# A written-out order for the first part of a fused recurrence and gated-MLP kernel: the state's matmuls as a step of their own, a read of the banks in place of a drain, 48-row loads

## The chip, the cores and the metric

The kernel runs on one core of a Trainium2 chip. The metric is device microseconds (us) of one execution; lower is better. Shown are the median of three runs and one execution taken with the hardware profiler.

## The reference

A gated linear recurrence over time feeds a gated MLP.

```python
B, H, S, D = 4, 8, 768, 48
for t in range(S):
    kt, vt, rt = k[:, :, t], v[:, :, t], r[:, :, t]
    cur = einsum('bhd,bhe->bhde', u[None] * kt, vt)
    y[:, :, t] = einsum('bhd,bhde->bhe', rt, state + cur)
    state = w[None, :, :, None] * state + einsum('bhd,bhe->bhde', kt, vt)
x = y.transpose(0, 2, 1, 3).reshape(B * S, H * D)          # 3072 x 384
gate = 1 / (1 + exp(-(x @ w_gate)))                         # 384 x 1536
out = (gate * (x @ w_val)) @ w_out                          # 1536 x 384
```

## The kernel before

**Tiling.** Time is cut into 12 chunks of 64 steps; a chunk has two groups of heads (`GROUPS`, numbered 0 to 23: chunk 0 is groups 0 and 1, chunk 1 is groups 2 and 3, and so on). Two chunks make a token tile of 512 columns, 256 from each. The MLP's 1536 hidden units come in 12 slices f of 128. A weight arrives as 64-bit words; ScalarE and VectorE turn it into a 32-bit value, which is split into a high and a low part, so each product of the MLP takes three matmuls.

**Steps.** In the first part (groups 0 to 7 and 14 items of MLP work) the string `START` gives the order of every step. Each engine has its own in-order queue, so the order in the string is the order on each engine. After it comes a loop over the rest, which this change touches only through the loads and through shared functions. A step's name is a letter and a number; the number is the group n, the slice f, or the item i. The names used here are these.

- SyncE's queue issues the loads: `L.n` channels (r and k of group n, 512 KB), `X.n` tokens (k and v, 400 KB), `W.f` weights (1152 KB, slice 0 in two halves), `F.n` six small copies (`fills`) that rearrange x inside SBUF.
- TensorE: `Z.n` scores, 64 small matmuls. `I.n` apply: from chunk 1 on 32 matmuls from the state (`from_state`), then 32 from the scores, into the same two banks. `O.n` the state's update, 32 matmuls. `U.i` up-projection of item i, `D.i` down-projection of item i, `tt` a table turned round.
- VectorE: `k`, `Rv` (scaled keys and queries), `K` (keep: scores under a mask into SBUF), `s` (add to the state), `l` (the low part of x), `j` (join the words of a weight slice, three instructions), `ov` (the low part of the weights), `Tv` (scaled token keys), `m` (gate times value), `qv` (the low part of h).
- ScalarE: `A` (bonus keys), `c`, `w` (scale the words, high part of the weights), `d` (decay the state), `h` (the high part of x), `g` (sigmoid), `H` (the high part of h), `tn`.
- GpSimd: the same as `Rv`, `Tv`, `ov`, `qv` under the names `R`, `T`, `o`, `q`.

Items 0 and 2 use weight slice 0, items 1 and 3 slice 1: items 0 and 1 work on the 256 columns of chunk 0, items 2 and 3 on those of chunk 1. Items 4 to 13 use slices 2 to 11 on all 512 columns. So U.0 needs the x of groups 0 and 1 and the copies F.0, and U.2 needs the x of groups 2 and 3 and the copies F.2.

**Buffers.** The ring of PSUM banks has three: an apply takes two, an up-projection takes two one after the other, and each waits for the readers of the bank's last tenant. The scores have one pair of banks. Channel loads rotate through three buffers.

**The drain.** In the first part an apply is `from_state`, then `nc.tensor.drain()`, then the matmuls from the scores. In the later part the next group's scores and the outer products stand between the two halves, and two one-column copies of the banks into `seen` (line 374) set the order.

Of the kernel before, what the change touches and what calls it, by code (L numbers as in the profile page):

```python
# [9 lines left out]
F32 = mybir.dt.float32  # L10
# [21 lines left out]
GROUPS = [(c, g) for c in range(NC) for g in (1, 0)]  # L32
# [4 lines left out]
HALF, FIRST = 2, 8  # L37
# [1 line left out]


START = """
L.0 tc A.0 tk ti.1 tp W.0 X.0 k.0 Rv.0 c0.0 ti.0 c0.1 L.1 j0.1 A.1 Z.0 K.0 tt L.2 k.1 I.0 Rv.2 A.2
R.1 X.1 tn h.0 T.0 X.3 Z.1 k.2 T.1 l.0 L.3 K.1 O.0 s.0 j0.0 W.1 A.3 I.1 w0.1 o0v.1 h.1 l.1 L.4 R.3
w0.0 c.1 X.2 F.0 Z.2 K.2 W.2 o0.0 O.1 s.1 j.1 Tv.3 X.6 U.0 g.0 c.2 m.0 I.2 k.3 w.1 W.4 W.7 ov.1 d.2
T.2 O.2 h.2 l.2 X.4 s.2 H.0 Z.3 K.3 A.4 q.0 k.4 R.4 c.4 j.2 U.1 g.1 I.3 O.3 L.7 L.5 m.1 d.3 h.3 H.1
l.3 A.5 D.0 w.2 R.5 Z.4 T.4 s.3 K.4 F.2 U.2 k.5 g.2 m.2 q.1 D.1 H.2 U.3 g.3 Z.5 j.4 m.3 X.5 I.4 O.4
W.3 L.6 T.5 H.3 d.4 R.6 X.7 ov.2 h.4 q.3 q.2 c.3 K.5 W.5 s.4 w.4 l.4 U.4 j.3 D.2 g.4 m.4 A.6 H.4 D.3
ov.4 qv.4 w.3 I.5 O.5 d.5 W.6 h.5 c.5 D.4 k.6 ov.3 l.5 c.6 s.5 U.5 A.7 g.5 j.5 w.5 U.6 g.6 j.6 w.6
ov.5 c.7 Z.6 m.5 m.6 K.6 U.7 H.5 qv.5 W.9 g.7 j.7 H.6 D.5 qv.6 o.6 I.6 Tv.6 w.7 W.8 k.7 d.6 D.6 O.6
m.7 Rv.7 H.7 s.6 h.6 c.8 l.6 ov.7 U.8 g.8 q.7 F.6 j.8 c.9 j.9 D.7 w.8 U.9 g.9 ov.8 Z.7 W.11 m.9 w.9  # L50
U.10 H.9 m.8 W.10 H.8 qv.8 D.8 g.10 o.9 K.7 q.9 D.9 m.10 I.7 c.11 j.11 c.10 H.10 qv.10 D.10 h.7 T.7
d.7 j.10 w.10 O.7 l.7 s.7 U.11 w.11 ov.10 g.11 ov.11 U.12 m.11 H.11 F.7 g.12 m.12 q.11 H.12 q.12 D.11
U.13 g.13 D.12 m.13 H.13 q.13
"""


# [1 line left out]
def rwkv_then_moe(ctx: ExitStack, tc: tile.TileContext, wd, ch, tk, rt, ut, wt, rk0, vn0, wd0, out):  # L58
    nc = tc.nc
# [19 lines left out]
    def one_bank():  # L79
        return ring.tile([P, 512], F32, name="ring")  # L80
# [168 lines left out]
    xt, dec, ga, yb, kv = {}, {}, {}, {}, {}  # L249
    seen = const.tile([112, 2], F32, name="seen")  # L250
# [94 lines left out]

    def keep(n):
        sc, t = ga.pop(n), score[n % 2]
# [6 lines left out]
        for m, at in ((0, 0), (1, 256))[: 1 if n >= FIRST else 2]:  # L354
# [233 lines left out]
    def finish(i):  # L588
# [29 lines left out]
    for step in START.split():  # L618
        name, _, arg = step.partition(".")
# [16 lines left out]
    n = FIRST  # L636
# [51 lines left out]
    with tc.If(bad != 0):  # L688
        with ExitStack() as g:
# [3 lines left out]
            st = gp.tile([P, NP, B, D], F32, name="st")  # L693
# [18 lines left out]
            with tc.For_i(0, NC) as c:  # L712
                for p in range(NP):
                    nc.sync.dma_start(
                        out=rkc[:, p].rearrange("q a b i -> q (a b i)"),
                        in_=rk0[bass.ds(c, 1), p].rearrange("o q x -> (o q) x"),
                    )
                with tc.For_i(0, C) as i:
                    for lo, side in ((0, 1), (64, 0)):
# [18 lines left out]
                    for lo in (0, 64):  # L738
                        y = one_bank()
# [11 lines left out]
                    out=xg[bass.ds(c, 1)].rearrange("o q p t -> (o q) p t"),  # L751
                    in_=yc.rearrange("q p b i -> q p (b i)"),
# [119 lines left out]
```

## Time and profile before

| | us |
|---|---|
| median of three runs | 541.75 |
| lowest and highest | 540.87, 541.93 |
| the profiled execution | 540.73 |
| its span, first to last instruction | 538.9 |
| TensorE busy in the span | 518.4 (96%) |
| VectorE busy in the span | 216.4 (40%) |
| bytes moved by DMA | 48.03 MB |

A span is counted from the first instruction; the profiled execution's own time is 1.8 us more. Rows name a line of the kernel, an engine and the tiles by the program's names: `ring<-dec,state` is a matmul from the state, `ring<-score,toks` one from the scores, `ring<-xt,wx` an up-projection, `acc<-h,wx` a down-projection, `xt<-ring,xt` on VectorE the low part of x.

### The profile page before, as it was taken

The page shows a single profiled execution, that of the slowest core. Times are in us where ns is not written, and L with a number is a line of the kernel's source. Part 1 is how long each engine was busy: PE and PEld are TensorE (multiplying, and loading weights), DVE is VectorE, ACT ScalarE, POOL GpSimd, SP SyncE. Part 2 cuts the span into 40 slices and gives each one's busy share as a digit, 9 for nine tenths or more (in the row PEclk, how much of TensorE's full clock was granted, in tenths as well). Part 3 has the DMA queues.
Part 4 walks back from the last instruction along what each step waited for, and adds up shares of the span by engine and source line. Part 5 has one row for each costly group of instructions (what it writes and reads, how often), then busy time and mean ns, then how long its engine had stood idle before and what let it go on. Part 6 is the DMA issues. An engine that isn't in the chain of part 4 may idle for free.

```text
span 538.9 us, 12058 instructions
## 1 busy us (share of the span) xinstructions
PE 518.4 (96%) x5268; PEld 425.6 (79%) x5268; DVE 216.4 (40%) x375; ACT 171.3 (32%) x354; POOL 174.8 (32%) x159
## 2 busy tenths in 40 slices
PE   2889999999999999999999999999999999999996
PEld 2778878788788887888888888888888887888885
DVE  7999989912343342432413414313414311111111
ACT  5485755522132322231332222312322212221121
POOL 3424022122814444244145144143242311111120
PEclk9999999999999999999999999999999999999998
DMA  8895705053022214220303402203400001100001
GB/s 318 312 338 217 286 1 186 15 205 128 2 86 86 66 50 144 85 74 12 95 3 103 145 5 82 65 30 106 144 1 16 11 2 19 60 1 1 0 1 63
DMA packets 15706, 48.03 MB, mean 89 GB/s; under 512 B 2368, under 2 KB 5056, under 8 KB 14240
## 3 DMA queue, kind: packets, MB, share of 16 engines
q1 hardware_dynamic: 15360, 46.81, 25.4%
q8 instruction: 43, 0.70, 0.5%
q10 hardware_dynamic: 288, 0.39, 0.2%
q14 instruction: 15, 0.12, 0.1%
HBM read 40.12 MB, written 4.72 MB: 83 GB/s over the span
## 4 chain that ended last, share of the span: by engine, by line
PE 91%; DMA 4%; DVE 1%; SPq 1%; issue 1%; ACT 0%; POOL 0%; DVEq 0%; ACTq 0%; POOLq 0%
PE ring L495 56%; PE acc L533 27%; PE ring L313 5%; PE sc L341 2%; DMA xt<-xt 1%; DMA chan<-in_ch 1%; PE sc L396 1%; DMA wr<-in_wt 1%; SPq L457 1%; PE sc L533 1%; POOL dec L294 0%; DVE wf L236 0%; DVE wx L246 0%; ACT wx L243 0%; ACT wf L229 0%
## 5 line engine op out<-in xcount | busy, mean ns | idle before, releaser
L495 PE MATMUL ring<-xt,wx 128*128 128x512 f32 (+1 forms) x1332 | 316.4, 391 | 1.4 <-DMA xt<-xt 1.2
L495 PEld LDWEIGHTS ring<-xt,wx 128*128 128x128 f32 x1332 | 246.1, 190 | 56.6 <-issue 1.3
L517 POOL TENSOR_TENSOR h<-sg,h 128x512 fp32r<-128x512 f32 (+1 forms) x68 | 86.7, 1276 | 298.8 <-ACT h L513 298.8
L533 PE MATMUL acc<-h,wx 128*128 128x512 f32 (+1 forms) x666 | 161.1, 383 | 0.0
L508 DVE TENSOR_TENSOR sg<-ring,sg 128x512 f32<-128x512 f32 (+1 forms) x74 | 49.9, 676 | 275.6 <-PE ring L495 275.6
L533 PEld LDWEIGHTS acc<-h,wx 128*128 128x128 f32 x666 | 119.6, 188 | 24.4
L504 ACT ACTIVATE sg<-ring 128x512 f32<-128x512 f32 (+1 forms) x74 | 43.4, 587 | 184.3 <-PE ring L495 181.2
L513 ACT CAST h<-sg 128x512 fp32r<-128x512 f32 (+1 forms) x74 | 45.3, 613 | 112.0 <-DVE sg L508 111.1
L415 ACT ACTIVATE state<-state,every 112x96 f32<-112x96 f32 x80 | 23.5, 365 | 26.2 <-PE ring L313 26.2
L294 POOL TENSOR_TENSOR dec<-chan,every 128x512 f32<-128x512 f32 x21 | 25.9, 1233 | 17.0 <-DMA chan<-in_ch 12.7
L453 DVE TENSOR_TENSOR xt<-ring,xt 112x256 fp32r<-112x256 f32 (+1 forms) x52 | 20.0, 419 | 24.9 <-ACT xt L449 24.4
L341 PE MATMUL sc<-dec,chan 48*64 48x64 f32 x768 | 17.4, 231 | 7.9 <-DVE dec L294 7.9
L355 DVE COPY_PREDICATED score<-masks,sc 128x512 f32<-128x512 int32 x32 | 23.9, 745 | 1.5 <-PE sc L341 0.6
L449 ACT CAST xt<-ring 112x256 fp32r<-112x256 f32 (+1 forms) x52 | 17.1, 373 | 19.6 <-PE ring L313 17.0
L341 PEld LDWEIGHTS sc<-dec,chan 48*64 48x64 f32 x768 | 15.0, 145 | 9.3 <-DVE dec L294 7.9
L313 PE MATMUL ring<-score,toks 64*48 64x64 f32 (+1 forms) x768 | 18.7, 230 | 3.7 <-POOL dec L294 1.6
L304 POOL TENSOR_TENSOR toks<-toks,tabn 128x384 f32<-128x384 f32 x20 | 21.1, 1059 | 1.7 <-ACT tabn L194 1.6
L313 PEld LDWEIGHTS ring<-score,toks 64*48 64x48 f32 (+1 forms) x768 | 15.3, 133 | 5.1 <-POOL dec L294 1.8
L313 PEld LDWEIGHTS ring<-dec,state 48*48 48x48 f32 (+1 forms) x704 | 12.4, 127 | 8.3 <-issue 7.4
L300 DVE TENSOR_TENSOR chan<-chan,every 128x512 f32<-128x512 f32 x24 | 17.2, 715 | 0.9 <-ACT dec L273 0.9
L246 POOL TENSOR_TENSOR wx<-wf,wx 128x1152 fp32r<-128x1152 f32 (+1 forms) x3 | 6.8, 2262 | 31.9 <-ACT wx L243 31.9
L282 POOL TENSOR_TENSOR dec<-dec,toks 128x384 f32<-128x384 f32 x16 | 16.3, 1017 | 1.2
(61 smaller groups left out, 260.0 us busy)
## 6 DMA issues: line engine op xcount, KB each, us to landing
wr<-in_wt SPq DMA_DIRECT2D x11, 1152.0 KB, 8.0
chan<-in_ch SPq DMA_DIRECT2D x24, 512.0 KB, 4.9
toks<-in_tk SPq DMA_DIRECT2D x24, 400.0 KB, 5.0
out_y<-wf SPq DMA_DIRECT2D x16, 256.0 KB, 2.3
dec<-in_rt SPq DMA_DIRECT2D x16, 192.0 KB, 2.6
xt<-xt SPq DMA_DIRECT2D x30, 64.0 KB, 2.3
wr<-in_wt SPq DMA_DIRECT2D x2, 576.0 KB, 5.4
xt<-xt SPq DMA_DIRECT2D x12, 32.0 KB, 5.1
```

The source lines that it names most:

```text
L294: eng.tensor_tensor(v4(t[:, 0]), v4(chan[n][:, 0]), bc2(table_of(n)), ALU.mult)
L304: eng.tensor_tensor(v4(k), v4(k), bc2(tabn[:, 4 * g : 4 * g + 4]), ALU.mult)
L313: nc.tensor.matmul(yb[n][bank][64 * half : 64 * half + m, cs], lhsT, rhs, start=first, stop=stop, skip_group_check=True,)
L341: nc.tensor.matmul(sc[64 * gm : 64 * gm + 64, be ^ gm, o : o + C], kk[row, cs : cs + C], rr[row, cs : cs + C], start=True, stop=True,)
L355: nc.vector.copy_predicated(t.rearrange("q (b m i) -> q b m i", b=2, m=4), masks[:, m].bitcast(I32).unsqueeze(1).unsqueeze(1).broadcast_to ...
L415: nc.scalar.activation(st[:, p, s], st[:, p, s], AF.Copy, scale=pw[0:112, 4 * g + 2 * p + s, 64:65],)
L495: nc.tensor.matmul(o[:, self.cols], w[a][:, g * DM + kt * P : g * DM + (kt + 1) * P], self.x[:, kt, b, self.cols], start=(k == 0), stop=(k ...
L504: nc.scalar.activation(sg[:, c], self.pair[f][0][:, c], AF.Sigmoid)
L508: nc.vector.tensor_tensor(sg[:, c], self.pair.pop(f)[1][:, c], sg[:, c], ALU.mult)
L513: nc.scalar.copy(out=h[:, 0, c], in_=sg[:, c])
L517: eng.tensor_tensor(h[:, 1, c], self.sg.pop(f)[:, c], h[:, 0, c], ALU.subtract)
L533: nc.tensor.matmul(acc[:, to], w[a][:, 2 * DM + d * P : 2 * DM + (d + 1) * P], h[:, b, cols], start=(f == 0 and k == 0 and self.cols.start ...
```

## The change

Four things change. (1) The 32 matmuls from the state become a step `S.n` for groups 2 to 7; a step `e.n` (on VectorE) or `ea.n` (on ScalarE) copies one column of each of the two banks into `seen`; `I.n` then does only the matmuls from the scores, and the drain stays for the very last group alone. (2) From the fourth on, a channel load moves rows 0 to 47 and 64 to 111 in two transfers of 192 KB instead of all 128 rows in one; the three buffers are handed out in the order in which the scores give them back. (3) `add_state` of groups 0 and 1 copies on ScalarE (`sa`) instead of VectorE (`s`). (4) `START` is written anew.

```diff
-L.0 tc A.0 tk ti.1 tp W.0 X.0 k.0 Rv.0 c0.0 ti.0 c0.1 L.1 j0.1 A.1 Z.0 K.0 tt L.2 k.1 I.0 Rv.2 A.2
-R.1 X.1 tn h.0 T.0 X.3 Z.1 k.2 T.1 l.0 L.3 K.1 O.0 s.0 j0.0 W.1 A.3 I.1 w0.1 o0v.1 h.1 l.1 L.4 R.3
-w0.0 c.1 X.2 F.0 Z.2 K.2 W.2 o0.0 O.1 s.1 j.1 Tv.3 X.6 U.0 g.0 c.2 m.0 I.2 k.3 w.1 W.4 W.7 ov.1 d.2
-T.2 O.2 h.2 l.2 X.4 s.2 H.0 Z.3 K.3 A.4 q.0 k.4 R.4 c.4 j.2 U.1 g.1 I.3 O.3 L.7 L.5 m.1 d.3 h.3 H.1
-l.3 A.5 D.0 w.2 R.5 Z.4 T.4 s.3 K.4 F.2 U.2 k.5 g.2 m.2 q.1 D.1 H.2 U.3 g.3 Z.5 j.4 m.3 X.5 I.4 O.4
...
+tk ti.1 tp L.0 tc A.0 W.0 k.0 Rv.0 Z.0 c0.0 tt j0.0 L.1 W.1 c0.1 A.1 X.0 j0.1 tn ti.0 L.3 k.1 K.0 L.2
+R.1 Tv.0 w0.1 I.0 c.1 O.0 w0.0 Z.1 X.1 h.0 T.1 sa.0 W.2 j.1 l.0 K.1 W.4 I.1 o0v.0 A.2 o0v.1 Rv.2 O.1
+A.3 k.3 k.2 h.1 c.2 Z.2 l.1 j.2 sa.1 w.1 R.3 F.0 U.0 K.2 X.4 g.0 X.2 m.0 S.2 w.2 H.0 X.3 e.2 T.3 Z.3
+T.2 q.0 I.2 ov.1 d.2 T.4 O.2 s.2 W.8 h.2 l.2 U.1 g.1 S.3 L.4 L.6 A.4 L.5 K.3 e.3 I.3 d.3 m.1 Rv.4 W.3
+O.3 k.4 H.1 s.3 h.3 F.2 D.0 l.3 o.2 c.4 c.3 Z.4 L.7 q.1 D.1 U.2 g.2 A.5 j.4 m.2 R.5 U.3 H.2 g.3 k.5
+S.4 ea.4 X.7 W.11 q.2 D.2 K.4 I.4 O.4 m.3 H.3 w.4 d.4 X.5 j.3 h.4 T.5 w.3 s.4 l.4 A.6 Z.5 U.4 g.4
+ov.3 q.3 K.5 m.4 S.5 ov.4 D.3 ea.5 I.5 d.5 O.5 s.5 H.4 R.6 X.6 h.5 l.5 W.5 c.5 qv.4 A.7 R.7 W.6 U.5
...
-    ach = main.enter_context(tc.tile_pool(name="ach", bufs=3))
+    ach = main.enter_context(tc.tile_pool(name="ach", bufs=1))
...
+    CHANNELS = slice(0, D), slice(64, 64 + D)
     chan, toks = {}, {}
+    cbuf = [ach.tile([P, 2, 512], F32, name=f"chan{i}") for i in range(3)]
 
     def load_channels(n):
         c, g = GROUPS[n]
-        chan[n] = ach.tile([P, 2, 512], F32, name="chan")
-        nc.sync.dma_start(out=chan[n], in_=ch[c, g])
+        whole = len(chan) < 3
+        chan[n] = cbuf.pop(0)
+        for rows in (slice(0, P),) if whole else CHANNELS:
+            nc.sync.dma_start(out=chan[n][rows], in_=ch[c, g, rows])
...
+        cbuf.append(chan[n])
...
+    def states_part(n):
+        yb[n] = one_bank(), one_bank()
+        from_state(n)
+
+    def see(n, copy=nc.vector.tensor_copy):
+        for b in range(2):
+            copy(out=seen[:, b : b + 1], in_=yb[n][b][0:112, 0:1])
+
     def apply(n):
         c, g = GROUPS[n]
         v, t = toks[n][:, 1], score[n % 2]
-        yb[n] = one_bank(), one_bank()
-        if c:
-            from_state(n)
-            if n < FIRST or n + 1 == len(GROUPS):
+        if n not in yb:
+            if c:
+                states_part(n)
+            else:
+                yb[n] = one_bank(), one_bank()
+            if n + 1 == len(GROUPS):
                 nc.tensor.drain()
-            else:
+            elif c:
                 scores(n + 1)
                 if GROUPS[n][0] < NC - 1:
                     outer(n, ga[n + 1][:, :, 256:512])
-                for b in range(2):
-                    nc.vector.tensor_copy(seen[:, b : b + 1], yb[n][b][0:112, 0:1])
+                see(n)
...
-    def add_state(n):
+    def add_state(n, copy=nc.vector.tensor_copy):
...
-                nc.vector.tensor_copy(st[:, :, s], y)
+                copy(out=st[:, :, s], in_=y)
...
+        "S": states_part, "e": see, "ea": lambda n: see(n, nc.scalar.copy),
+        "sa": lambda n: add_state(n, nc.scalar.copy),
```

The orders on TensorE that follow, up to U.4, are these.

```
before: Z.0 tt I.0 Z.1 O.0 I.1 Z.2 O.1 U.0 I.2 O.2 Z.3 U.1 I.3 O.3 D.0 Z.4 U.2 D.1 U.3 Z.5 I.4 O.4 U.4
after:  Z.0 tt I.0 O.0 Z.1 I.1 O.1 Z.2 U.0 S.2 Z.3 I.2 O.2 U.1 S.3 I.3 O.3 D.0 Z.4 D.1 U.2 U.3 S.4 D.2 I.4 O.4 Z.5 U.4
```

And on VectorE, up to l.3.

```
before: tk ti.1 tp k.0 Rv.0 ti.0 j0.1 K.0 k.1 Rv.2 k.2 l.0 K.1 s.0 j0.0 o0v.1 l.1 K.2 s.1 j.1 Tv.3 m.0 k.3 ov.1 l.2 s.2 K.3 k.4 j.2 m.1 l.3
after:  tk ti.1 tp k.0 Rv.0 j0.0 j0.1 ti.0 k.1 K.0 Tv.0 j.1 l.0 K.1 o0v.0 o0v.1 Rv.2 k.3 k.2 l.1 j.2 K.2 m.0 e.2 ov.1 s.2 l.2 K.3 e.3 m.1 Rv.4 k.4 s.3 l.3
```

## Rows read from the trace of the kernel before

**Rows 1.** Windows: busy us and instructions of each engine, PEclk, DMA share, GB/s

```profile
0.00:39.24 39.24, 25.00 (x717) 22.94 (x718) 34.29 (x62) 23.76 (x58) 13.39 (x24) 1.00 0.88 327
39.24:525.00 485.76, 484.47 (x4507) 395.28 (x4508) 179.65 (x310) 145.34 (x293) 160.08 (x135) 1.00 0.22 71
```

**Rows 2.** Timeline of TensorE: the first three up-projections (start us, us)

```profile
23.02 4.21 PE L495 MATMUL ring<-xt,wx 128*128 128x256 f32 x18
...
30.35 2.39 PE L495 MATMUL ring<-xt,wx 128*128 128x256 f32 x18 [0.19 <-DVE wx L246]
...
39.24 2.53 PE L495 MATMUL ring<-xt,wx 128*128 128x256 f32 x18 [1.18 <-DMA xt<-xt]
```

**Rows 3.** The chain that ended last, 31 to 43 us (start us, us)

```profile
31.69 7.41 DMA xt<-xt
...
41.77 1.08 PE acc L533 x9
```

**Rows 4.** Timeline of TensorE: the two halves of an apply, groups 4, 5 and 8

```profile
45.90 0.63 PE L313 MATMUL ring<-dec,state 48*64 48x64 f32 x27
46.96 0.32 PE L313 MATMUL ring<-dec,state 48*64 48x64 f32 x5 [0.43 <-issue]
47.39 0.68 PE L313 MATMUL ring<-score,toks 64*64 64x64 f32 x32
...
55.00 0.68 PE L313 MATMUL ring<-dec,state 48*64 48x64 f32 x32
55.86 0.68 PE L313 MATMUL ring<-score,toks 64*64 64x64 f32 x32 [0.18 <-issue]
...
150.98 0.68 PE L313 MATMUL ring<-dec,state 48*64 48x64 f32 x32
151.47 0.65 PE L341 MATMUL sc<-dec,chan 48*64 48x64 f32 x32
```

**Rows 5.** Timeline of VectorE: one of each kind of step

```profile
12.16 0.68 DVE L300 TENSOR_TENSOR chan<-chan,every 128x512 f32<-128x512 f32 x1
...
15.32 1.49 DVE L355 COPY_PREDICATED score<-masks,sc 128x512 f32<-128x512 int32 x2 [0.60 <-PE sc L341]
16.71 0.60 DVE L428 COPY state<-ring 112x192 f32<-112x192 f32 x2
...
20.22 1.74 DVE L453 TENSOR_TENSOR xt<-ring,xt 48x256 fp32r<-48x256 f32 x4
...
23.91 0.76 DVE L235 TENSOR_SCALAR wf<-wf 128x1152 int32<-128x1152 int32 x1
24.71 1.36 DVE L236 SCALAR_TENSOR_TENSOR wf<-wr,wf 128x1152 int32<-128x1152 int32 x1
26.10 1.36 DVE L237 SCALAR_TENSOR_TENSOR wf<-wr,wf 128x1152 int32<-128x1152 int32 x1
27.37 0.55 DVE L304 TENSOR_TENSOR toks<-toks,tabn 128x384 f32<-128x384 f32 x1
27.84 0.42 DVE L508 TENSOR_TENSOR sg<-ring,sg 128x256 f32<-128x256 f32 x1
...
28.94 1.36 DVE L246 TENSOR_TENSOR wx<-wf,wx 128x1152 fp32r<-128x1152 f32 x1
...
37.29 1.72 DVE L453 TENSOR_TENSOR xt<-ring,xt 48x256 fp32r<-48x256 f32 x4
```

**Rows 6.** The tile seen: instruction, count, ns min/median/max, first and last start

```profile
L374 DVE COPY seen<-ring x30: 147/148/149, 151.8 to 426.8; 112x1 f32<-112x1 f32 x30
```

**Rows 7.** SyncE's timeline, and the six-copy steps' time to landing (tile xt)

```profile
31.05 4.95 SPq L457 DMA_DIRECT2D xt<-xt  x6
...
DMA to landing us min/median/max: 2.5/5.1/7.8
```

**Rows 8.** ScalarE's timeline (end of W.0's landing), and the window 5 to 10 us

```profile
8.06 0.73 ACT L229 ACTIVATE wf<-wr 128x576 f32<-128x576 f32 x1 [0.71 <-DMA wr<-in_wt]
...
5.00:10.00 5.00, 2.11 (x80) 2.11 (x83) 3.89 (x7) 2.73 (x6) 0.00 (x0) 1.00 1.02 414
```

More of the change, by code (lines that the diff above doesn't have):

```diff
@@ L41 @@
 START = """
-L.0 tc A.0 tk ti.1 tp W.0 X.0 k.0 Rv.0 c0.0 ti.0 c0.1 L.1 j0.1 A.1 Z.0 K.0 tt L.2 k.1 I.0 Rv.2 A.2
-R.1 X.1 tn h.0 T.0 X.3 Z.1 k.2 T.1 l.0 L.3 K.1 O.0 s.0 j0.0 W.1 A.3 I.1 w0.1 o0v.1 h.1 l.1 L.4 R.3
-w0.0 c.1 X.2 F.0 Z.2 K.2 W.2 o0.0 O.1 s.1 j.1 Tv.3 X.6 U.0 g.0 c.2 m.0 I.2 k.3 w.1 W.4 W.7 ov.1 d.2
-T.2 O.2 h.2 l.2 X.4 s.2 H.0 Z.3 K.3 A.4 q.0 k.4 R.4 c.4 j.2 U.1 g.1 I.3 O.3 L.7 L.5 m.1 d.3 h.3 H.1
-l.3 A.5 D.0 w.2 R.5 Z.4 T.4 s.3 K.4 F.2 U.2 k.5 g.2 m.2 q.1 D.1 H.2 U.3 g.3 Z.5 j.4 m.3 X.5 I.4 O.4
[L47 to L53, printed above, removed]
+tk ti.1 tp L.0 tc A.0 W.0 k.0 Rv.0 Z.0 c0.0 tt j0.0 L.1 W.1 c0.1 A.1 X.0 j0.1 tn ti.0 L.3 k.1 K.0 L.2
[5 more added lines that the diff above has]
+ov.3 q.3 K.5 m.4 S.5 ov.4 D.3 ea.5 I.5 d.5 O.5 s.5 H.4 R.6 X.6 h.5 l.5 W.5 c.5 qv.4 A.7 R.7 W.6 U.5
+g.5 j.5 c.6 D.4 W.9 Tv.6 U.6 k.6 m.5 w.5 ov.5 j.6 W.7 c.7 H.5 g.6 w.6 k.7 U.7 Z.6 m.6 qv.5 D.5 g.7
+ov.6 H.6 q.6 K.6 S.6 ea.6 m.7 Z.7 j.7 I.6 d.6 O.6 H.7 qv.7 s.6 h.6 l.6 w.7 ov.7 c.8 j.8 T.7 c.9 W.10
+D.6 j.9 D.7 U.8 g.8 w.8 ov.8 U.9 g.9 m.8 H.8 U.10 K.7 w.9 o.9 qv.8 D.8 m.9 g.10 H.9 m.10 q.9 S.7 c.10
+D.9 H.10 e.7 I.7 O.7 d.7 qv.10 h.7 j.10 s.7 D.10 l.7 U.11 w.10 ov.10 c.11 j.11 g.11 m.11 U.12 w.11
+H.11 qv.11 ov.11 g.12 m.12 D.11 H.12 q.12 F.7 U.13 g.13 D.12 F.6 m.13 H.13 qv.13
 """
@@ L600, in rwkv_then_moe @@
         "k": keys, "T": token_keys, "Z": scores, "K": keep, "I": apply, "O": outer,
-        "d": decay_state, "s": add_state, "h": x_high, "l": x_low, "F": fills, "D": finish,
+        "S": states_part, "e": see, "ea": lambda n: see(n, nc.scalar.copy),
+        "d": decay_state, "s": add_state, "sa": lambda n: add_state(n, nc.scalar.copy), "h": x_high, "l": x_low, "F": fills, "D": finish,
         "tc": constants, "tk": channel_table, "ti": inverses, "tp": token_powers,
```

## The prediction

> **What bounds the kernel now.** I read the windows first. From 39.24 us on TensorE is busy 484.47 of 485.76 us: there the time is the sum of its matmuls, and nothing that another engine does shortens it. Before 39.24 it is busy 25.00 of 39.24, while VectorE is busy 34.29 [rows 1]. So the order of the steps can gain in two places: by how far TensorE's list of work has come when it stops waiting, and by the small gaps after that. I take U.2 as the mark, the last start with a long wait ahead of it: it begins at 39.24, 1.18 after its engine was free, and what it waited for is the copies F.2, which landed 7.41 us after their first issue [rows 2, 3]. Before it, U.1 begins at 30.35 the moment VectorE has ov.1 ready [rows 2]: VectorE paces the front part.
>
> Next the gaps behind the mark. Where the drain stands, the first matmul from the scores begins 0.86 us after the first from the state (group 5); without a drain the next 32 matmuls begin 0.49 after (group 8). Group 4 takes 1.49, with an idle 0.43 amid its state matmuls that no engine released [rows 4].
>
> **VectorE up to l.1, which U.0 needs.** Before, l.1 ends at 20.22 + 1.74 = 21.96 [rows 5]. The new order puts ahead of it j.1 (three instructions, 23.91 to 27.37: 3.46), k.3 (about 0.6, as successive steps overlap a little), Tv.0 (0.5) and the half-slice o0v.0 (half of 1.36: 0.7), and takes away s.0 (0.5): 4.75 more. VectorE idled 0.60 before K.1; a queue this full probably has no such gap: 4.15, so l.1 ends at 26.1 (26.7 with the gap) [rows 5]. O.1, which stood between l.1 and U.0, now runs earlier. U.0 starts at 26.1, about 3.1 later than before [rows 2].
>
> **VectorE up to l.3, which U.2 needs.** Before, l.3 ends at 37.29 + 1.72 = 39.0. Added ahead of it: Tv.0 0.5, o0v.0 0.7, Rv.4 0.6, s.3 0.5, and e.2 and e.3, four copies of 0.147 (0.6 in all). Taken away: s.0, s.1, Tv.3, 0.5 each. Net +1.4, less the lost gap of 0.6: 39.8 at the earliest [rows 5, 6]. It will wait some for TensorE and ScalarE (m.1 for U.1, s.3 for O.3, l.3 for h.3): between 0 and 2.5 us, and I take 1.1, so 40.9.
>
> The state copies sa.0 and sa.1 cost ScalarE about what they cost VectorE (0.6 each [rows 5]); ScalarE is busy only 23.76 of the first 39.24 us [rows 1], and that idle time hides them. If it were gone, h.1, w.1 and U.0's second bank would be 0.6 later.
>
> **TensorE up to the mark.** U.0 from 26.1 takes 4.21 if it runs as slowly as now, to 30.3. Then come S.2 0.5, Z.3 1.1, I.2 0.5, O.2 0.55, U.1 2.4, S.3 0.5, I.3 and O.3 1.05, D.0 1.1, Z.4 1.1, D.1 1.1, together 9.9 [rows 2 to 4]: 40.2. K.2 now stands behind j.2: 26.1 + 3.46 + 1.4 = 31.0, and Z.3 needs its bank, 0.2 late. I.3 waits for e.3, which is queued behind K.3: I allow 0.3. That gives 40.7.
>
> **The copies F.2.** Between l.2 and l.3 VectorE has 5.5 us of its own work, so l.2 ends near 34.4. F.2's six issues take 4.95 on SyncE's queue and a copy needs at least 2.5 to land [rows 7]: last landing 41.2, or 39.9 if the issues take 0.6 each, as all but the first would with nothing to wait for. They must not stand behind bulk loads: the loads up to W.4 are 7336 KB, of which 1672 KB are in at 8.06, and at the 414 GB/s of this stretch the rest is in at 22.1 [rows 8]. The fills F.0 are issued after that. W.8, two channel groups and W.3 follow, some 12 us of traffic that starts near 24 and ends near 36, ahead of F.2's last issue.
>
> No 48-row transfer stands in the trace. Two of 192 KB take 0.95 us at 414 GB/s, against 1.3 for the 512 KB now [rows 8]; at most each takes as long as the whole does now, 2.5 for both. I take 1.0 (it is the same traffic with fewer bytes), which hides behind VectorE's queue anyway; the upper end puts F.2 about 1 us later. The Trainium skill (SBUF — State Buffer, Door 1: The DMA port swizzle) says that rows 0 to 63 reach only half of the ports, so a 48-row transfer would run at half rate: 1.9 for both, a loss instead of a gain. No row of before shows it; by it the sum stays and the late fills below become likelier.
>
> So three paths meet at the mark: 40.7, 40.9 and 39.9 to 41.2. I take 40.9, with 39.8 and 42.5 as ends. D.1 (1.08 [rows 3]) is done before U.2 now and came after it before, so 39.24 + 1.08 = 40.3 would be even. **Term one: +0.6** (-0.5 to +2.2).
>
> **Behind the mark.** Group 4 loses its drain and its idle 0.43: 1.49 - 0.49 = 1.0 (0.57 if that idle time comes back, since no engine released it). Groups 5, 6 and 7 lose 0.86 - 0.49 = 0.37 each, 1.1 [rows 4]. The reads of the banks cost TensorE nothing there: D.2, D.3, Z.7 and D.9 stand between S and I, 1.1 to 2.1 us, against two copies of 0.15 [rows 6]. With that cover gone each would cost about what the drain did, 0.4. **Term two: -2.1** (-1.7 at least).
>
> One new wait: j.3 now stands ahead of s.4 and l.4. From l.3 at 40.9 VectorE does j.4, m.2, k.5, K.4, m.3, j.3, s.4, l.4: 10.9, to 51.8. TensorE reaches U.4's second bank, which l.4 must release, at 40.9 + 10.4 = 51.3. **Term three: +0.3** (0 to 0.8). Everything after is TensorE's list, unchanged; the halved channel issues of the later part hide behind its 420 us of matmuls.
>
> **Sum:** 0.6 - 2.1 + 0.3 = -1.2. On the profiled 540.73 that is 539.5. Its time is 1.0 below the median of the runs, 541.75, so the forecast for a median is 540.5.
>
> **Rivals.**
> *No gain (22%).* Either the fills land late or VectorE waits longer, and U.2 starts at 42.0: 1.7 - 2.1 + 0.3 = -0.1, 541.6. For it: F.2's copies now need 7.41 with bulk traffic ahead [rows 3], and W.3 is again queued just before. Against it: that traffic is out by my count. Or the 0.86 is the change of operands and not the drain, so that groups 5 to 7 give nothing back: 0.6 - 1.0 + 0.3, 541.6 as well; the idle 0.18 in the row speaks against that [rows 4].
>
> *Slower (18%): TensorE stays slow longer.* U.0's 18 matmuls take 4.21 and U.1's 2.39, with a granted clock of 1.00 shown for both: 256 columns in 234 ns, the 1.2 GHz level, against 133 ns, near 2.4 GHz [rows 1, 2]. It rose during 4 us without a gap in U.0. In the new order I see TensorE idle before I.0, before I.1 and before Z.2. If the rise comes only after U.1, S.2, I.2, O.2, Z.3 and U.1 take 3.5 to 4 us longer, the mark is at 44.3, and the time is 541.75 + 4.0 - 2.1 + 0.3 = 543.9. It decides from a mark at 42.1 on. Against it: U.0 is as long a stretch as before, with more matmuls just ahead. The Trainium skill (TensorE: Matmul & The Clock Gate, Part 1) says that idle time throttles the array to half and that sustained work releases it; the trace's U.0 and U.1 agree (4.21 and 2.39), and by that rule this rival's price is the one to fear when the front has more gaps.
>
> *More gain (15%).* The clock is up before U.0 ends (up to 1.9 less on TensorE's path), VectorE never waits, and the fills land in time: the mark at 39.8, no wait at U.4: -0.5 - 2.1 = -2.6, 539.1.
>
> **How the numbers follow.** The forecast case has 45%, with its own range of 539.5 to 541.5. A measurement of this kernel can tell about 0.2%, 1.1 us. The forecast lies close to that bound: of its 45, 31 are faster and 14 within it. With the 15 of the larger gain: faster 0.46. Within: 14 and 16 of the no-gain case, 0.30. Slower: 6 of that case and 18, 0.24. The range takes in 1.2 below the larger gain, for gaps in the front that I can't see closing, and most of the slow-clock case: 537.9 to 543.6.
>
> **What would show it.** After: U.0 near 26 and l.1 ending just before it; U.1 near 33; U.2 near 41 with D.1 ahead of it; state and score matmuls of groups 4 to 7 apart by whole other steps, with no idle time before the second half; a short wait in the middle of U.4; from there on the same list. Wrong if U.2 starts before 39.8 or after 42.5, if U.1 takes 4 us, or if S.n or I.n waits for a read of the banks.

## The result, and the profile after

The changed kernel is slower: median 547.70 us (546.40 to 548.87, four runs) against 541.74 (540.87 to 541.93, four runs), a ratio of 1.0109 with a 95% interval of 1.0086 to 1.0131. The forecast was 540.5 in a range of 537.9 to 543.6; the time is 4.1 above the range's upper end, on the side that had a chance of 0.24. The profiled execution took 546.75, with a span of 545.0.

The windows of the changed kernel, columns as in [rows 1]: the stretch up to before's U.2 first, then three of 4 us.

```profile
0.00:39.24 39.24, 21.67 (x600) 19.83 (x601) 33.03 (x59) 22.10 (x54) 14.85 (x23) 1.00 0.91 301
...
12.00:16.00 4.00, 1.44 (x58) 1.47 (x61) 3.84 (x7) 1.85 (x3) 1.74 (x1) 1.00 1.04 311
...
32.00:36.00 4.00, 3.00 (x70) 2.63 (x70) 2.07 (x6) 1.38 (x5) 4.00 (x4) 1.00 1.03 219
36.00:40.00 4.00, 2.69 (x103) 2.28 (x102) 2.90 (x7) 2.64 (x9) 1.51 (x1) 1.00 1.04 235
```

Two things stand out beside [rows 1]. In the first 39.24 us TensorE has done 3.3 us less (21.67 against 25.00). And where 48-row loads are under way, the DMA engines show a full share (1.03 to 1.04) but move 219 to 311 GB/s; before, a share of 1.02 went with 414 [rows 8].

TensorE's timeline (start, time, line, operation, idle time before it with its releaser), from U.0 to U.4:

```profile
25.60 4.21 PE L509 MATMUL ring<-xt,wx 128*128 128x256 f32 x18
...
33.29 0.67 PE L317 MATMUL ring<-toks 64*64 64x48 f32 x32 [0.62 <-POOL toks L308]
33.89 1.34 PE L509 MATMUL ring<-xt,wx 128*128 128x256 f32 x9
35.51 1.30 PE L509 MATMUL ring<-xt,wx 128*128 128x256 f32 x9 [0.28 <-DVE xt L467]
36.74 0.68 PE L317 MATMUL ring<-dec,state 48*64 48x64 f32 x32
37.72 0.63 PE L317 MATMUL ring<-score,toks 64*64 64x64 f32 x20 [0.30 <-DVE seen L372]
39.35 0.38 PE L317 MATMUL ring<-score,toks 64*48 64x64 f32 x11 [1.01 <-issue]
...
40.08 2.20 PE L547 MATMUL acc<-h,wx 128*128 128x256 f32 x9
...
45.09 4.43 PE L509 MATMUL ring<-xt,wx 128*128 128x256 f32 x36
...
53.35 4.45 PE L509 MATMUL ring<-xt,wx 128*128 128x512 f32 x18
```

These rows answer [rows 2] and [rows 4]. U.0 starts at 25.60 (26.1 was forecast), U.1 at 33.89, U.2 at 45.09 where 40.9 was forecast. Between S.3 and U.2 lie a wait for the read of the banks (0.30), an idle 1.01 in the middle of I.3 that no engine released, and a D.0 that takes 2.20 where new_whole (below) has 1.35. The last is the clock, which one-microsecond windows of TensorE show (busy time, instructions, granted clock, DMA share, GB/s):

```profile
40.00:41.00 1.00, 1.00 (x17) 0.60 0.93 374
41.00:42.00 1.00, 1.00 (x7) 0.50 1.04 232
42.00:43.00 1.00, 1.00 (x30) 0.50 0.31 80
43.00:44.00 1.00, 1.00 (x49) 0.69 0.13 34
```

From 40.2 to 43.6 the granted clock is 0.50, the 1.2 GHz level, after gaps at 37.4 and 38.35 to 39.35; D.0 and Z.4 run in it, and D.1, from 43.92, no longer does.

They alone do not decide U.2. SyncE's timeline with F.2, and the time to landing of its six copies in the view of the tile xt (window 35 to 41):

```profile
35.72 4.79 SPq L471 DMA_DIRECT2D xt<-xt  x6
...
DMA to landing us min/median/max: 5.4/7.1/8.6
```

Issued from 35.72 to 39.92, they land from 44.3 to 45.3, the first 0.2 behind W.3, a whole load that was issued at 32.81 behind the six 48-row transfers and took 11.3 to land. U.2 needs these copies, so it could not have begun before 44.3 without the stall and the low clock either.

The chain that ended last names what held O.2, answering [rows 3]:

```profile
25.12 4.89 DMA toks<-in_tk
30.20 3.05 POOL toks L308 x2
```

The tokens of X.3 landed at 30.0. GpSimd runs T.3 and then T.2 (two of 1.5 each), and O.2 waits for T.2, whose own tokens were not the late ones.

Two more places, from TensorE's timeline: U.10, and the start of the last nine down-projection matmuls, by which I compare kernels below (531.70 in before, read from the same row of its timeline).

```profile
95.12 4.46 PE L509 MATMUL ring<-xt,wx 128*128 128x512 f32 x18 [1.04 <-DVE sg L522]
...
535.21 1.90 PE L547 MATMUL acc<-h,wx 128*128 128x512 f32 x9
```

**The account on the span**, 545.0 against 538.9, so +6.1 where -1.2 was forecast. U.2 would be even at 40.3, so the mark is 4.8 late (forecast 0.6). From the mark to the last nine the list regains 1.3 (535.21 - 531.70 = 3.5; forecast 1.8). From the last nine to the end it takes 9.8 against 7.2: +2.6, which the forecast did not have.

### The profile page after: what moved, and what is told of

It is laid out like the page before. It is cut to its first block, busy times and chain, and to the rows that moved or that the text cites. A ratio compares the mean times of both kernels' runs of the same rounds, so it can differ in the third digit from the quotient of the medians.

```text
span 545.0 us, 12130 instructions
## 1 busy us (share of the span) xinstructions
PE 518.6 (95%) x5268; PEld 426.1 (78%) x5268; DVE 216.7 (40%) x380; ACT 172.4 (32%) x364; POOL 172.5 (32%) x156
## 4 chain that ended last, share of the span: by engine, by line
PE 89%; DMA 4%; DVE 3%; issue 1%; ACT 1%; POOL 1%; SPq 0%; POOLq 0%; DVEq 0%; ACTq 0%
PE ring L509 53%; PE acc L547 26%; PE ring L317 5%; PE sc L345 2%; DMA wr<-in_wt 2%; PE sc L410 1%; DMA toks<-in_tk 1%; DVE wf L240 1%; PE sc L547 1%; DMA chan<-in_ch 1%; POOL toks L308 1%; DVE wx L250 0%; DVE wf L239 0%; DVE sg L522 0%; ACT dec L277 0%
## 5 line engine op out<-in xcount | busy, mean ns | idle before, releaser
L531 POOL TENSOR_TENSOR h<-sg,h 128x512 fp32r<-128x512 f32 (+1 forms) x66 | 84.8, 1285 | 309.7 <-ACT h L527 294.4
L518 ACT ACTIVATE sg<-ring 128x512 f32<-128x512 f32 (+1 forms) x74 | 43.3, 586 | 179.2 <-PE ring L509 178.4
L527 ACT CAST h<-sg 128x512 fp32r<-128x512 f32 (+1 forms) x74 | 45.3, 612 | 107.7 <-DVE sg L522 105.7
L317 PE MATMUL ring<-score,toks 64*64 64x64 f32 (+1 forms) x768 | 18.8, 229 | 8.0 <-DVE score L360 6.4
L240 DVE SCALAR_TENSOR_TENSOR wf<-wr,wf 128x1152 int32<-128x1152 int32 (+1 forms) x13 | 16.5, 1266 | 0.4
```

Source lines behind the costliest of these rows:

```text
L317: nc.tensor.matmul(yb[n][bank][64 * half : 64 * half + m, cs], lhsT, rhs, start=first, stop=stop, skip_group_check=True,)
L518: nc.scalar.activation(sg[:, c], self.pair[f][0][:, c], AF.Sigmoid)
L527: nc.scalar.copy(out=h[:, 0, c], in_=sg[:, c])
L531: eng.tensor_tensor(h[:, 1, c], self.sg.pop(f)[:, c], h[:, 0, c], ALU.subtract)
```

## The experiments

The theory was that the 48-row loads are slow for their bytes and that their lateness opens the gaps; the rivals were that the new order by itself is late (theory "order"), that the read of the banks is what costs, and that the drain was never worth what the prediction gave for it.

**new_whole: the new kernel with all channel loads whole.**

```diff
-        whole = len(chan) < 3
+        whole = True
```

> The changed kernel, with every channel load moving all 128 rows again. Theory 1 (48-row transfers run at about half the rate, and their late landing is what holds up the front): L.4 lands some 1.5 us earlier than at 37.2, A.4 no longer keeps d.3, h.3 and H.1 waiting, TensorE has no idle time near 38 and its clock does not fall at 40; U.2 near 42, span about 541 to 543. Rival (the new order itself is late, by VectorE's queue and the token loads behind W.2 and W.4): within 1 us of the changed kernel, U.2 at 44 to 45.5, U.10 still waits for VectorE near 95. If the long end of the changed kernel (last matmul to end of span 7.5 us against 5.0) comes from the larger number of issues, it goes back to 5.0 here.

Measured 543.36 (542.33 to 545.25), ratio 1.0026 (1.0012 to 1.0040). So by the ratios 0.0083, 4.5 of the 5.9 us that the change costs, go with the row ranges of the loads. Its windows and TensorE's timeline:

```profile
12.00:16.00 4.00, 1.28 (x50) 1.31 (x54) 3.84 (x7) 1.98 (x3) 1.74 (x1) 1.00 1.06 421
...
32.00:36.00 4.00, 2.44 (x73) 2.08 (x63) 2.06 (x5) 1.47 (x6) 4.00 (x4) 1.00 1.04 413
```

```profile
33.69 0.67 PE L317 MATMUL ring<-toks 64*64 64x48 f32 x32 [1.26 <-POOL toks L308]
...
38.13 0.72 PE L317 MATMUL ring<-score,toks 64*64 64x64 f32 x31 [0.30 <-DVE seen L372]
...
39.25 1.35 PE L547 MATMUL acc<-h,wx 128*128 128x256 f32 x9
...
42.80 4.43 PE L509 MATMUL ring<-xt,wx 128*128 128x256 f32 x36
```

The same traffic share moves 413 and 421 GB/s in the stretches that had 219 and 311. The stall in I.3 and the low clock are gone, and U.2 is 2.3 earlier. F.2's copies, issued from 36.12 to 39.30, now land 2.9 to 4.9 later, from 41.1 to 42.2, again right behind W.3 (40.9), and U.2 starts without a wait. What is left, 1.4 us, goes with the rest of the change, the order above all: O.2 waits 1.26 for T.2, and U.10 1.02.

**old_48: the kernel before with the 48-row loads alone** (the same loop over `CHANNELS` and the hand-out of buffers, `START` as before).

> The kernel before, in its own order, with only the 48-row channel loads. Theory 1 (half rate): L.3, L.4, L.7 and L.5 take 0.5 to 1 us longer each; F.2, which is queued behind L.7 and L.5, lands about 1 us later, and U.2 starts at 40 to 40.5: slower by 0.5 to 1.5 us. Rival (same traffic with a quarter fewer bytes): U.2 0.3 to 0.6 us earlier, 541.0 to 541.7. By both the part behind 48 us is unchanged, but for the end if that hangs on the number of issues.

Measured 544.61 (543.42 to 546.21), ratio 1.0038 (1.0023 to 1.0053): 2.1 us by the ratio. So the loads are a loss in either order, and a larger one in the new. (The hand-out of the buffers was not tried without them in the old order; new_whole keeps it.) A window of it, SyncE's timeline with F.2, and U.2:

```profile
12.00:16.00 4.00, 3.41 (x125) 3.44 (x125) 3.38 (x7) 2.25 (x8) 2.44 (x3) 1.00 1.04 318
```

```profile
31.84 9.06 SPq L462 DMA_DIRECT2D xt<-xt  x6
```

```profile
41.11 4.19 PE L500 MATMUL ring<-xt,wx 128*128 128x256 f32 x18 [2.27 <-DVE score L360]
```

F.2's six issues take 9.06 instead of 4.95 [rows 7], and U.2 starts 1.9 later than before [rows 2]. Its row names K.4, whose first half ended just then; but in the kernel before U.2 (39.24) starts ahead of K.4 (39.57), so it does not need it. F.2's first two copies, issued at 31.84 and 32.49, took 8.9 and 8.5 to land, which is at 40.8 and 41.0. After that gap U.2 too runs at a granted clock of 0.56 in the window 40 to 44.

**new_64 and new_fix_112: other row ranges.** The first is the changed kernel with halves of 64 rows, the second is new_fix (below) with one transfer of rows 0 to 111.

```diff
-    CHANNELS = slice(0, D), slice(64, 64 + D)
+    CHANNELS = slice(0, 64), slice(64, P)
```

> The changed kernel with its split loads as two transfers of 64 rows (0 to 63, 64 to 127) instead of two of 48: all bytes again, in two issues. Theory 1 (a transfer that reaches only partitions of one half of SBUF runs at half rate): while these loads run, 32 to 40 us, the DMA share is 1.0 at about 210 to 230 GB/s; the loads take a third longer than with 48 rows, L.4 lands near 38.5, and the time is that of the changed kernel or up to 2 us more, 547 to 549.5. Rival (the slow rate comes from three rows for each of the 16 DMA engines, or from the bytes of a transfer): about 400 GB/s in that stretch, and the time of the new order with whole loads, 543 to 544.

> The same, with the channel loads from the fourth on as one transfer of rows 0 to 111 (448 KB): fewer bytes, but both halves of the partitions in one transfer. Theory 1 (what made the 48-row loads slow is that a transfer reaches one half only): about 400 GB/s while they run, and within 0.4 us of the same kernel with whole loads. Rival (any row count other than 128 is slow): under 350 GB/s at a full DMA share near 32 to 40 us, and 1 to 4 us slower.

Measured: new_64 549.96 (549.22 to 550.96), ratio 1.0132 (1.0109 to 1.0155); new_fix_112 546.28 (542.78 to 548.77), ratio 1.0069 (1.0045 to 1.0094), against 0.9989 for new_fix. The windows of new_64, then those of new_fix_112:

```profile
32.00:36.00 4.00, 3.02 (x117) 2.62 (x108) 2.07 (x5) 1.90 (x8) 4.00 (x4) 1.00 1.03 235
36.00:40.00 4.00, 2.69 (x71) 2.31 (x74) 3.27 (x8) 1.98 (x7) 2.16 (x1) 1.00 1.08 257
```

```profile
32.00:36.00 4.00, 3.72 (x138) 3.50 (x128) 3.13 (x6) 2.37 (x8) 3.66 (x3) 1.00 1.03 275
36.00:40.00 4.00, 3.67 (x111) 3.21 (x109) 3.22 (x9) 2.59 (x10) 1.40 (x1) 1.00 1.03 292
```

Two halves of 64 rows carry all the bytes and are no faster than two of 48, so it isn't that the transfers have fewer bytes. A single transfer of 112 rows moves 275 to 292 GB/s, so it isn't the number of transfers alone either, nor only that a transfer stays in one half of the rows. In both, U.2 waits for F.2's copies: 3.26 in new_64 (start 47.53) and 2.92 in new_fix_112 (start 45.49).

**old_split: the kernel before with the state's matmuls as a step of their own** for groups 4 to 7, ordered by ScalarE's read.

```diff
-... U.3 g.3 Z.5 j.4 m.3 X.5 I.4 O.4
+... U.3 g.3 S.4 Z.5 ea.4 j.4 m.3 X.5 I.4 O.4
-... A.6 H.4 D.3 ... H.6 D.5 qv.6 o.6 I.6 ... q.9 D.9 m.10 I.7 c.11 j.11 c.10 H.10
+... A.6 S.5 ea.5 H.4 D.3 ... H.6 S.6 D.5 ea.6 qv.6 o.6 I.6 ... q.9 S.7 D.9 m.10 c.11 j.11 c.10 ea.7 I.7 H.10
```

> The kernel before, in its own order, with the state's matmuls of groups 4 to 7 as a step of their own ahead of Z.5, D.3, D.5 and D.9, and a read of the banks by ScalarE in place of the drain. Theory (the second term of the prediction: each drain costs 0.37, group 4 up to 1.0, and the read costs TensorE nothing where another step stands between): faster by 1.5 to 2.2 us, 539.5 to 540.2, no idle time ahead of the second halves. Rival (the time between the two halves is a change of operands, or comes back as a wait for the read): within 0.4 us of the kernel before.

Measured 541.95 (540.88 to 542.87), ratio 1.0004 (0.9989 to 1.0018): no gain clear of noise (the interval leaves room for 0.6), where term two gives 2.1. In the profiled execution the weights W.2 took 6.9 to land, against 5.3 before, so that U.1 starts 2.09 late and D.1 at 43.03 (41.61 before), all of it ahead of the first changed step. The last nine start at 532.65, 0.95 behind before, so some 0.5 came back behind D.1. Group 5 on TensorE's timeline:

```profile
53.89 1.24 PE L543 MATMUL acc<-h,wx 128*128 128x256 f32 x9
55.05 0.68 PE L313 MATMUL ring<-dec,state 48*64 48x64 f32 x32
55.67 1.34 PE L543 MATMUL acc<-h,wx 128*128 128x256 f32 x9
56.93 0.68 PE L313 MATMUL ring<-score,toks 64*64 64x64 f32 x32
```

From D.2 to I.5 that is 56.93 - 53.89 = 3.04. Before, D.2 and D.3 run in one piece from 52.77 (2.31 for eighteen matmuls), and I.5's second half starts at 55.86 [rows 4]: 3.09. The idle 0.18 is gone, but each passage between 48-row and 128-row matmuls costs something: S.5 takes 0.62 to the next start, not 0.49, and D.3 takes 1.26 to the next start where half of D.2 and D.3 in one piece takes some 1.1.

**new_whole_drain: new_whole with the steps S, e and ea taken out and the drain put back.**

```diff
-            if n + 1 == len(GROUPS):
+            if c and (n < FIRST or n + 1 == len(GROUPS)):
                 nc.tensor.drain()
```

> The new order with whole loads, but with the state's matmuls back beside those from the scores and the drain between them; no reads of the banks. The prediction's second term (a step of its own saves 0.37 in each group): 1.5 to 2.2 us slower than the new order with whole loads. Theory 2 (it saves 0.37 only where scores, small matmuls too, stand between, groups 2 and 6; where a down-projection stands between, groups 4, 5 and 7, the change from small to large matmuls and back costs 0.1 to 0.2 each way and eats it; in group 3 the read costs 0.3): 0.3 to 0.8 us slower.

Measured 543.95 (543.35 to 544.75), ratio 1.0032 (1.0019 to 1.0046). It is 0.6 above new_whole by the medians and 0.3 by the ratios, whose intervals overlap; the last nine start at 533.74 against 533.35. Here the order is the same, so stretches can be set side by side. Group 6, new_whole first and then new_whole_drain:

```profile
76.99 0.68 PE L317 MATMUL ring<-dec,state 48*64 48x64 f32 x32
...
78.42 0.65 PE L317 MATMUL ring<-score,toks 64*48 64x64 f32 x32
...
79.45 1.89 PE L547 MATMUL acc<-h,wx 128*128 128x512 f32 x7
```

```profile
78.39 0.64 PE L317 MATMUL ring<-dec,state 48*64 48x64 f32 x32
79.20 0.68 PE L317 MATMUL ring<-score,toks 64*64 64x64 f32 x32 [0.17 <-issue]
...
80.26 2.11 PE L547 MATMUL acc<-h,wx 128*128 128x512 f32 x8
```

| stretch on TensorE | with S | with drain |
|---|---|---|
| group 4, U.2 to I.4 | 49.44 - 42.80 = 6.64 (6.25 in the changed kernel) | 49.73 - 43.09 = 6.64 |
| group 5, U.4 to I.5 | 57.72 - 51.45 = 6.27 | 58.16 - 51.75 = 6.41 |
| group 6, Z.6 to D.6 | 79.45 - 73.64 = 5.81 | 80.26 - 74.06 = 6.20 |
| group 7, D.8 to D.10 | 103.66 - 97.53 = 6.13 | 104.08 - 97.97 = 6.11 |

So the step pays where small matmuls (Z.7) stand between its halves, 0.39, and next to nothing where a down-projection does. The 0.39 is then lost again: U.10 waits 1.02 for m.8 in new_whole and 0.64 in new_whole_drain, and starts 0.42 earlier, as the step before group 6 did.

**old_read: the kernel before with the read on VectorE in place of the drain, and nothing between.**

```diff
-                nc.tensor.drain()
+                see(n)
```

> The kernel before, in its own order, with VectorE's read of the two banks where the drain stood in groups 2 to 7, and nothing between the halves. Theory (the read waits its turn in VectorE's queue): group 2 +0.4, group 3 +2.6 (the read stands behind j.2, which ends near 37), group 5 +0.8, groups 4, 6 and 7 about as before; U.2 1 to 2 us later, slower by 2 to 4 us in all. Rival (the read is two copies of 0.15 us and costs about what the drain does): within 0.6 us of the kernel before.

Measured 550.06 (548.86 to 552.83), ratio 1.0152 (1.0116 to 1.0189): 8 us slower. TensorE's timeline around I.3:

```profile
36.83 1.18 PE L313 MATMUL ring<-score,toks 64*64 64x64 f32 x32 [3.01 <-DVE seen L367]
...
38.76 2.29 PE L545 MATMUL acc<-h,wx 128*128 128x256 f32 x9
```

The two copies of 0.15 stand behind all that VectorE has in its queue. I.2 waits 1.30 for them, I.3 3.01, I.5 1.14, and after the 3.01 the clock falls. The loss is twice the largest that was expected: U.2 is 3.3 late (42.52) and the last nine 8.4 (540.13), and the rest of the way to there is not followed here. So the read is cheap only with a step between, and only if its engine gets to it in time; in the new order it cost 0.30 at I.3 and nothing at I.4 to I.7.

**old_sa and old_sa_split4: is VectorE what paces the front?** The first moves the state copies of groups 0 and 1 to ScalarE in the old order, the second adds S.4 and ea.4 around Z.5.

```diff
-... O.0 s.0 j0.0 ... O.1 s.1 j.1 ...
+... O.0 sa.0 j0.0 ... O.1 sa.1 j.1 ...
```

> The kernel before, with one part of the change: the state of groups 0 and 1 is copied by ScalarE instead of VectorE. If VectorE paces the front, as the prediction says, ov.1 ends 1.0 us earlier and U.1 starts at 29.4 instead of 30.35, l.2 and with it the copies F.2 come 1 us earlier, U.2 near 38.2 to 38.5: faster by 0.6 to 1.0 us, 0.1 to 0.2%. Rival (the front waits for its loads: W.2 for ov.1 by way of ScalarE's queue, F.2 behind the bulk loads): U.1 and U.2 within 0.3 us of before, no change.

> The same, and the state's matmuls of group 4 as a step of their own ahead of the scores Z.5, with a read by ScalarE: the one place in the old order where a step of small matmuls can stand between the halves. Theory 2: another 0.4 us, up to 0.8 if the idle 0.43 in the state's matmuls of group 4 does not come back; 0.2 to 0.3% faster than the kernel before in all. Rival: no more than the kernel with the ScalarE copies alone, or no change at all.

Measured: old_sa 542.26 (540.70 to 543.47), ratio 1.0000 (0.9986 to 1.0013); old_sa_split4 541.79 (540.51 to 543.02), ratio 0.9988 (0.9975 to 1.0001). One microsecond less on VectorE changes nothing that the runs can tell. U.2 in old_sa, and a place in old_sa_split4:

```profile
39.69 3.84 PE L495 MATMUL ring<-xt,wx 128*128 128x256 f32 x18 [1.67 <-DMA xt<-xt]
```

```profile
47.60 0.28 PE L341 MATMUL sc<-chan,dec 48*64 48x64 f32 x3 [0.76 <-issue]
```

U.2 still waits for F.2's copies, longer than before [rows 2]: their landing sets the mark, not VectorE. After that wait the granted clock is 0.50 from 41 to 43, and U.2 takes 3.84; in old_sa_split4 it waits 1.63 and takes 2.52. Z.5 behind S.4 stalls 0.76 after its 58th matmul; old_split has an idle 0.22 at the next one.

**new_fix: the two waits of the new order mended.** On top of whole loads, T.2 before T.3 with its tokens first, and ov.8, m.8, H.8 ahead of j.9.

```diff
-... X.4 g.0 X.2 m.0 S.2 w.2 H.0 X.3 e.2 T.3 Z.3 / T.2 q.0 ...
+... X.2 g.0 X.3 m.0 S.2 w.2 H.0 X.4 e.2 T.2 Z.3 / T.3 q.0 ...
-... D.6 j.9 D.7 U.8 g.8 w.8 ov.8 U.9 g.9 m.8 H.8 U.10 ...
+... D.6 D.7 U.8 g.8 w.8 ov.8 m.8 H.8 j.9 U.9 g.9 U.10 ...
```

> The new order with whole loads, with two places of the order mended: the token loads go X.2, X.3, X.4 and T.2 goes ahead of T.3 on GpSimd; and VectorE does ov.8 and m.8 ahead of j.9. Theory (the order's own loss against before, 1.65 us at the last matmul, lies in those two waits: O.2 for T.2, 1.26, and U.10 for m.8, 1.02): both waits gone, U.2 near 41.6, no wait ahead of U.10, 1.5 to 2.3 us faster than the new order with whole loads; 0 to 0.2% faster than the kernel before. Rival (the front is held by several queues at once, and U.2 or a later step only waits for the next of them): under 1 us faster, still slower than before.

Measured 541.32 (540.72 to 543.14), ratio 0.9989 (0.9975 to 1.0003). TensorE's timeline:

```profile
31.76 0.69 PE L345 MATMUL sc<-dec,chan 48*64 48x64 f32 x32 [1.19 <-DVE score L360]
...
42.31 3.96 PE L509 MATMUL ring<-xt,wx 128*128 128x256 f32 x30
...
83.42 12.75 PE L509 MATMUL ring<-xt,wx 128*128 128x512 f32 x54
```

Both waits are gone: O.2 follows without a gap and U.8 to U.10 are one piece. It is 2.0 below new_whole by the medians, but U.2 comes only 0.5 earlier, where 1.2 was expected. A new wait stands 1.9 us ahead of the one that went (31.76 against 33.69), at Z.3 for K.2, which is queued behind j.2; j.2's last instruction took 2.04 there and 1.36 in new_whole, while GpSimd was at T.2 and T.3 (27.41 to 30.93), which the mended order starts 3.1 us earlier. It and old_sa_split4 are the lowest of all versions, and neither is shown to be faster than the kernel before: their intervals reach 1.0003 and 1.0001.

**after_again: the changed kernel, one more execution.**

> The changed kernel once more, one profile. If the idle microsecond amid I.3, the fall of the clock near 40 us and the long end (9.6 us from the start of the last six matmuls) belong to the program, they are all there again; if they belong to the execution, one or more differ.

Measured 545.54. TensorE's timeline:

```profile
38.66 0.72 PE L317 MATMUL ring<-score,toks 64*64 64x64 f32 x31 [0.30 <-DVE seen L372]
...
43.68 0.36 PE L509 MATMUL ring<-xt,wx 128*128 128x256 f32 x1 [0.20 <-DMA xt<-xt]
44.53 4.31 PE L509 MATMUL ring<-xt,wx 128*128 128x256 f32 x35 [0.49 <-issue]
```

No stall in I.3 and no low clock (D.0, at 39.79, takes 1.34), and yet U.2 runs only from 44.53, first held by F.2's landing. The stall and the clock belong to an execution and not to the program; the late loads are there each time, with F.2's first two copies at 43.3 and 43.5. Its last nine start at 534.68, 3.0 behind before.

## Why the prediction was wrong, point by point

**The step that failed is the price of the 48-row loads, and with it the landing of F.2.** It read: "I take 1.0 (it is the same traffic with fewer bytes), which hides behind VectorE's queue anyway; the upper end puts F.2 about 1 us later." Neither half holds. At a full DMA share they go with 219 to 235 GB/s where whole loads have 413. The three groups that are issued from 26 to 32.8 (SyncE's timeline, in new_whole to 32.5 too) are 1.18 MB, an estimated 5.2 us at 227 GB/s, against 1.57 MB and 3.8 us whole at 413: fewer bytes and a longer time, 1.7 for a group's two transfers where 1.0 was taken and 2.5 was the upper bound. And it does not hide. The prediction had the bulk traffic end near 36 and F.2 land by 39.9 to 41.2; the traffic ahead of F.2 ended with W.3 at 44.1 (40.9 in new_whole), and F.2's copies landed behind it, from 44.3 to 45.3. A.4 also waits 1.65 for its channels (37.30 against 35.93 in new_whole), but s.3 behind it waits for O.3 and not for A.4, so that delay was not on the path. Taking the row ranges away gives back 4.5 of 5.9 us by the ratios (new_whole), and adding them to the old order costs 2.1 (old_48).

The sentence beside it cited the Trainium skill (SBUF — State Buffer, Door 1: The DMA port swizzle), by which a transfer within rows 0 to 63 reaches half of the ports. The trace agrees in direction for 48 and 64 rows (219 to 257 against 413 GB/s), and I should have given the late fills more than their 22%. It doesn't explain 112 rows, which lie in both halves and move 275 to 292.

**VectorE's walk to U.0** was right: 26.1 forecast, 25.60 measured, with l.1 ending at 25.25.

**Term one**, +0.6, measured +4.8. Of the 4.2 missed, 2.3 go with the loads (45.09 against 42.80 in new_whole) by way of F.2, whose copies land at 44.3 at the earliest; the stall and the low clock can have added 0.8 at most, and after_again without them has its last nine 0.5 earlier. The other 1.9 (42.80 against 40.9) are the order's own: mostly O.2's 1.26 behind T.3 and T.2, an operand that the sum did not follow although the moved X.2 and X.3 stand in the new string. The sum "9.9" on TensorE took O.2 as free to run. That the mark had "three paths" was right; that VectorE was the one to beat was not: old_sa relieves it and gains nothing. The 7.41 that the prediction counts from F.2's first issue runs from the second (31.69, not 31.05 [rows 3, 7]), which changes nothing in the sum. But it read "VectorE paces the front part" out of U.1's row; the chain of the kernel before has ahead of that ov.1 a load, whose words ScalarE (from 26.54) and then VectorE wait for:

```profile
21.17 5.26 DMA wr<-in_wt
```

**Term two**, -2.1, is right only as a net. Behind the mark the forecast was -2.1 + 0.3 = -1.8. new_fix regains 1.8 there (its U.2 is 2.0 behind the even 40.3, its last nine at 531.87 only 0.2), the changed kernel 1.3, new_whole 0.85 (2.5, then 1.65), since the wait at U.10, 1.02 to 1.04, eats part. But the credit was misplaced. With the order held fixed the step saves 0.14 in group 5, 0.39 in group 6, none in group 7 and 0 to 0.39 in group 4 (0.39 only by setting the changed kernel beside another execution), 0.5 to 0.9 in all; group 4's idle 0.43 is absent in the new order with the drain too (48.88 to 49.73 in new_whole_drain is 0.85, not 1.49). It is most likely one of the stalls of the last section, and not the drain's. And in the old order the split alone gives nothing that can be told from noise (old_split). The rival "the 0.86 is the change of operands and not the drain" was nearer for groups 5 and 7; the 0.18 that I held against it is real, but it is bought back by two more passages between small and large matmuls.

**Term three**, +0.3 in U.4: not seen. U.4 is one piece of 4.45. The new wait is at U.10, where m.8 stands behind j.8, j.9 and ov.8; the prediction walked VectorE's queue to U.4 and stopped there.

**The reads of the banks** behaved as priced, 0.30 at I.3 and none later. By the prediction's own list, U.2 after 42.5 and a wait of I.n for a read were to show it wrong; both came.

**The rivals.** "No gain" named the mechanism, late fills, and gave it a mark of 42.0; it is 42.3 to 43.1 with whole loads, where U.2 starts without a wait, and 44.5 to 45.1 with 48-row loads, where the fills land from 43.3 to 45.3. "Slower" looked for the low clock at U.0 and U.1, where it was as before (4.21, then 2.64 for U.1's two halves); it came later, after the gaps at I.3, and drew D.0 to U.2 out by 1.5 in one execution (5.01 against 3.55 in new_whole), most of which F.2 would have cost anyway, and not in another.

**The end** is unexplained. From the last nine to the end of the span it takes 7.2 to 8.5 us in the eight profiles with whole loads and 8.3 to 9.8 in the five with other row ranges. The last stores land 4.5 and 3.8 us after their issue in the changed kernel and 2.9 and 2.8 before. No experiment changed the end by itself, old_sa has 8.5 at an unchanged median, and a link to the loads was not shown.

## What to carry to other kernels

Price a transfer by its rows and not only by its bytes: with the DMA engines fully busy, fewer rows here meant fewer GB/s, and a load cut from 128 to 96 rows took longer. Then look at what is queued behind it: F.2's small copies landed only when the bulk load ahead of them had, 0.2 behind W.3. When steps are put in a new order, follow each of them back to its operands on every queue, to the end of the rewritten stretch and not to one mark: two steps on the wrong side of a neighbour (T.3 before T.2, j.9 before m.8) cost 2 us, about what the removed drains were to save. Credit for a removed drain is to be counted from start to start with what will stand between, and measured with the order held fixed.

## What the runs showed of the hardware

- **GB/s at a DMA share of 1.03 or more**, by the rows of the channel loads, other traffic included, in the windows 32 to 40 us (12 to 16 us in brackets): 128 rows 413 (421) in new_whole; 112 rows 275 and 292 (327); 64 + 64 rows 235 and 257 (290); 48 + 48 rows 219 and 235 (311), in after_again 249 and 258 (337), in old_48 320 in 32 to 36 (318). In the same changed kernel, the windows 16 to 20 and 28 to 32, in which whole loads of weights and tokens come in, have 411 and 405. Why 112 rows are so far below 128 stays open.
- **The granted clock can fall to 0.50 in the front** after a gap: after 1.01 with 0.30 just ahead of it in one execution of the changed kernel, after 1.67 in old_sa, 2.27 in old_48, 2.92 in new_fix_112, 3.01 in old_read and 3.26 in new_64. It did not fall after 1.26 in new_whole, 1.41 in after_again, 1.63 in old_sa_split4 or 2.09 in old_split (U.1 then 2.39). The Trainium skill (TensorE: Matmul & The Clock Gate, Part 1) has idle time throttling the array; the runs agree that a fall follows a gap, and the length of the gap alone does not sort them.
- **Stalls that nothing released come at one instruction, and soon after a fetch of instructions.** I.3 stops after 20 matmuls in the changed kernel (1.01) and new_64 (0.86), and in old_sa (0.23) too; Z.5 behind S.4 in old_split (0.22) and old_sa_split4 (0.76); group 4's state matmuls in the kernel before (0.43), and U.2's second matmul in after_again (0.49). In after_again I.3 does not stop. In these seven the profile has a packet of the kind instruction (16 KB, queue q8) that ended 1.3 to 1.6 us before the stall did: at 37.8 for the changed kernel's 39.35, at 45.7 for the 46.96 of the kernel before. Where that packet came earlier, I.3 ran through (ended 35.8 in new_whole, 37.0 in after_again). So TensorE most likely waited for instructions; no experiment moved a packet, so this is not shown.
